# A long convolution by matmul: spectra stored in pairs of two words, first stage on 128 rows with a block-diagonal table

## The chip, the cores and the metric

The kernel runs on one core of a Trainium2 chip. A core has a matrix engine (TensorE, PE in the profile, with its weight loads shown apart as PEld), a vector engine (VectorE, DVE), a scalar engine (ScalarE, ACT), GpSimd (POOL), and queues for DMA transfers, here those of SyncE (SP) and ScalarE. The metric is device time in microseconds of one execution, lower is better; of the kernel before, three runs were timed.

## What is computed

A layer norm, a gated long convolution of 2048 positions over 512 channels, and an MLP behind a second layer norm:

```python
def _A_ref(q, k, v, shift_k, ssm_k, ssm_D):          # q is layernorm(x)
    ...
    for t in range(ks):                              # ks = 4
        k_shift = k_shift + k_pad[:, t:t + S, :] * shift_k[:, ks - 1 - t][None, None, :]
    kv = k_shift * v
    L = 2 * S
    ...                                              # zero padding to L, rfft of kv and of ssm_k
    y_f = kv_f * kf_f[None, :, :, :]
    y = irfft(y_f, L)[:, 0, :S, :]                   # shortened
    y = y + kv * ssm_D[None, None, :]
    return q * y
...
h = x + _A_ref(_layernorm(x, axis=-1), A_k, A_v, A_shift_k, A_ssm_k, A_ssm_D)
h2 = h + _B_ref(_layernorm(h, axis=-1), B_w1, B_w2)  # relu(z @ w1) @ w2, width 1376
```

## The kernel before

The Fourier transforms are written as matmuls in two stages each (a number of positions is split into 32 by 64). All instructions are issued in an order written out by hand; each engine works its own list in that order, and waits only for what it reads or overwrites.

*Setup (to about 16 us).* VectorE and ScalarE make sine and cosine tables. The small one, 64 columns, is kept as a sum of two bf16 tables, `f1hi` and `f1lo` (L192 to L195); a larger one, `st`, serves the second stage. `to_rows` (L217) transposes the filter with TensorE (L222) into `kfl`, whose partitions are four channel groups by 32 coarse positions, with 128 channels by 64 fine positions on each; here the moving operand is read 32 words apart. ACT and VectorE copy the result out of PSUM in turn.

*First stage (`stage1`, L230).* The 512 channels lie as four groups `rg` of 32 partitions. For each pair of channels and each `rg`, a matmul with 32 rows of weights (out of `kfl`, or `xfl` for the data) moves the 64 columns of `f1hi` or `f1lo`. The four `rg` use four row strips of the array side by side (`tile_position`). Eight calls each do 64 matmuls; each call fills two PSUM tiles of two banks, and each tile is written out by two instructions of 512 elements, one of VectorE and one of ScalarE (L248 and L250 for the filter, where `dmask` adds the direct term D, L252 and L253 for the data). For the data the moving table is padded to 128 columns (`wide`).

For the filter, `stage1` alternates with `taps` (L259): 8 matmuls of 512 columns for the four-tap shift convolution, and a product with `v` on VectorE (L266). Then the result is transposed by `to_rows` again, and `stage1` runs over it.

*The spectra.* The filter's are in `BK`, the data's in `BX`, both 16384 words of four bytes on each partition. A channel group g (0 to 63; each partition half holds one channel of the pair) and a first-stage frequency k1 (0 to 31) are found at

```python
BK = bkp.tile([P, 2, 2, DC, 32, 32], F32R, tag="K", name="BK")   # part, g // 32, rg, k1, g % 32
```

so 32 groups of the same k1 lie side by side, and two frequencies of the same group are 32 words (128 bytes) apart.

*Second stage and product.* `pairs(k1)` (L320) and `sums(k1)` (L329) multiply by the table `st` (or sums of it, `sm`). The weights are the tables, side by side in memory; the moving operand is one k1 of `BK` or `BX`, 256 columns: 8 runs of 32 words. `pairs` has 64 rows of weights, two matmuls at once; `sums` 128 rows. ScalarE copies the filter's part out of PSUM (`forms`, L317), and VectorE multiplies it with the data's part (`times`, L340), writing back over `BK` and `BX` at that k1. The sixteen rounds have two `pairs` and one `sums` each.

*Inverse, first stage (`inv1`, L446).* Here the spectra are the weights: for a group g the 128 weights are four `rg` by 32 k1, and they are read 32 words apart. The moving operand is a table of 256 columns (`inv3`, `inv12`). Four groups, 12 matmuls, fill one PSUM tile of two banks, of which there are three. Two copies take each tile out (L457): both by ScalarE for even blocks b, one by ScalarE and one by VectorE for odd ones. Between the sixteen blocks other work is issued: column means of `w1` on TensorE (`pm`, L434) and their subtraction on VectorE (L439), layer norm statistics and normalisation (L403, L424), and further tables.

*The rest.* When `inv1` has read `BK` for the last time its memory becomes `M`, and the loads of `w2` and of the second half of `x` start. `inv2` (L534), `gate` (L516) and the MLP (`mlp1`, L546, `mlp2`, L559) follow for four quarters of the positions.

Of the kernel before, what the change touches and what calls it, by code (L numbers as in the profile page):

```python
# [56 lines left out]
def kernel(  # L57
# [118 lines left out]
    _turns(nc, t3[:, 1, :], r3[:], n2c[:], 64, False)  # L176
    f1f = small([64], F32)
    _sin(f1f[:, 0:32], t1[:, 0:32], 128)
    _sin(f1f[:, 32:64], t1[:, 32:64], 128, neg=True)
# [20 lines left out]
    dmask = early.tile([P, DC, 64], BF16, name="dmask")  # L200
    nc.gpsimd.memset(dmask[:], 0.0)
    for dp in range(2):
        row = slice(64 * dp, 64 * dp + 1)
        nc.gpsimd.tensor_copy(out=dmask[row, :, :],
                              in_=draw[row, :].rearrange("p (r g d) -> p r g d", r=DC, d=2)[:, :, :, dp])
    nc.gpsimd.tensor_single_scalar(out=st[:, :, 128:192], in_=st[:, :, 0:64].bitcast(F32), scalar=-1.0, op=ALU.mult)
# [7 lines left out]
    def bank2(name):  # L214
        return psum.tile([P, 2, 512], F32, tag="ps", name=name)
# [13 lines left out]

    def stage1(fl, B, gb, dmul=None, wide=False):  # L230
        pss = [bank2("ps1") for _ in range(2)]
        for gi in range(8):
            g = 8 * gb + gi
            w = 128 if wide and gi < 7 else 64
            for f, first in ((f1hi, True), (f1lo, False)):
                for rg in range(4):
                    rows = slice(32 * rg, 32 * rg + 32)
                    nc.tensor.matmul(out=pss[rg // 2][:, rg % 2, 64 * gi:64 * gi + w],  # L238
                                     lhsT=fl[rows, 2 * g:2 * g + 2, :].rearrange("p d n -> p (d n)"),
                                     rhs=f[rows, 0:w], start=first, stop=not first,  # L240
                                     tile_position=(32 * rg, 0), skip_group_check=True)
        gs = slice(8 * gb, 8 * gb + 8)
        gh, gl = gb // 4, slice(8 * (gb % 4), 8 * (gb % 4) + 8)
        for h in range(2):
            rs = slice(2 * h, 2 * h + 2)
            pv = pss[h][:].rearrange("p r (g h c) -> p h r c g", h=2, c=32)
            if dmul is not None:
                nc.vector.tensor_tensor(out=B[:, 0, gh, rs, :, gl], in0=pv[:, 0],  # L248
                                        in1=dmul[:, rs, gs].unsqueeze(2).to_broadcast([P, 2, 32, 8]), op=ALU.add)
                nc.scalar.copy(out=B[:, 1, gh, rs, :, gl], in_=pv[:, 1])  # L250
            else:
                nc.scalar.copy(out=B[:, 0, gh, rs, :, gl], in_=pv[:, 0])  # L252
                nc.vector.tensor_copy(out=B[:, 1, gh, rs, :, gl], in_=pv[:, 1])  # L253

# [46 lines left out]
    BX = bxp.tile([P, 2, 2, DC, 32, 32], F32R, tag="X", name="BX")  # L301
    for gb in range(8):
        stage1(xfl, BX, gb, wide=True)
    pl.pop("psF")
# [15 lines left out]
    def pairs(k1):  # L320
        ps = psum.tile([P, 2, 512], F32, tag="u", name="u")
        for x, B in enumerate((BK, BX)):
            for i, t in ((0, st[:, k1, 64:192]), (1, st[:, k1, 0:128])):
                for dp, pq in enumerate(halves):
                    nc.tensor.matmul(out=ps[:, dp, 256 * x:256 * x + 256], lhsT=t[pq], rhs=B[pq, i, :, :, k1, :].rearrange("p h r l -> p (h r) l"),  # L325
                                     start=(i == 0), stop=(i == 1), tile_position=(64 * dp, 0), skip_group_check=True)
        return ps, forms(ps), BK[:, :, :, :, k1, :].rearrange("p s h r l -> p s (h r) l")

    def sums(k1):  # L329
        ps = psum.tile([P, 2, 512], F32, tag="u", name="us")  # L330
        for x, B in enumerate((BK, BX)):
            for j in range(2):
                for i in range(2):
                    nc.tensor.matmul(out=ps[:, j, 256 * x:256 * x + 256], lhsT=sm[:, i, k1 + j, :], rhs=B[:, i, :, :, k1 + j, :].rearrange("p h r l -> p (h r) l"),  # L334
                                     start=(i == 0), stop=(i == 1), skip_group_check=True)
        return ps, forms(ps), BX[:, 0, :, :, k1:k1 + 2, :].rearrange("p h r k l -> p k (h r) l")

    def times(unit):
        ps, kt, o = unit
        nc.vector.tensor_tensor(out=o, in0=ps[:, :, 256:512].rearrange("p s (x l) -> p s x l", l=32),  # L340
                                in1=kt[:].rearrange("p s (x l) -> p s x l", l=32), op=ALU.mult)

# [103 lines left out]
    def inv1(b):  # L446
        ps = psum.tile([P, 4, 2, 2, 64], F32, tag="ps", name="psi1")
        for i in range(4):
            g = 4 * b + i
            nc.tensor.matmul(out=ps[:, i].rearrange("p d a n -> p (d a n)"), lhsT=BX[:, 0, g // 32, :, :, g % 32].rearrange("p r k -> p (r k)"),  # L450
                             rhs=inv3[:].rearrange("p d a n -> p (d a n)"), start=True, stop=False, skip_group_check=True)
            for dp in range(2):
                nc.tensor.matmul(out=ps[:, i].rearrange("p d a n -> p (d a n)"),  # L453
                                 lhsT=BK[:, dp, g // 32, :, :, g % 32].rearrange("p r k -> p (r k)"),
                                 rhs=inv12[:, 2 - 2 * dp:6 - 2 * dp, :].rearrange("p a n -> p (a n)"),
                                 start=False, stop=(dp == 1), skip_group_check=True)
# [186 lines left out]
```

## Time and profile before

| | us |
|---|---|
| median of three runs | 250.69 (249.88 to 250.73) |
| the profiled execution | 252.94 |
| its span, first to last instruction | 251.2 |
| TensorE matmuls busy | 221.9 (88%), 2608 of them |
| TensorE weight loads busy | 160.8 (64%) |
| VectorE busy | 141.9 (56%) |
| ScalarE busy | 98.9 (39%) |
| GpSimd busy | 65.3 (26%) |
| mean granted TensorE clock | 0.955 of full |

Matmuls are pipelined, so a busy TensorE can still be waiting inside a matmul, for its weights for example; how far apart the starts of matmuls lie says more than the busy share. In the slices of the span, each a fortieth (6.28 us), a digit is the busy share in tenths:

```profile
PE   0579987758999997999999975999999999999992
PEld 0555447547888887899999975744474465444440
DVE  6859994764888885644533119307996228135031
ACT  3454443663777673243352200075027104504500
...
PEclk9999999997999998899999977599999999999998
```

The weight loads are densest from slice 16 to slice 23, which is `inv1`, and the granted clock falls at four places.

### The profile page before, as it was taken

To read this page: it belongs to the slowest core of one execution; us is meant where nothing else is said; L and a number is where in the kernel's file an instruction comes from. 1 tells how busy PE (TensorE), PEld (TensorE's weight loads), DVE (VectorE), ACT (ScalarE), POOL (GpSimd) and SP (SyncE) were. 2 spreads that over 40 slices of the span, in tenths; PEclk is the share of its full clock that TensorE was granted. 3 is DMA by queue.
4 is the path that set the end of the run, shared out by engine and by line. 5 is a ranking of instruction groups with operands and counts; after the bars stand their busy time and mean duration, and the time that the engine had idled before them with its cause. 6 is when DMAs were issued, how large, how long until landed. Compare 5 with 4: busy or idle time off the path is not lost.

```text
span 251.2 us, 6062 instructions
## 1 busy us (share of the span) xinstructions
PE 221.9 (88%) x2608; PEld 160.8 (64%) x2608; DVE 141.9 (56%) x236; ACT 98.9 (39%) x166; POOL 65.3 (26%) x80
## 2 busy tenths in 40 slices
PE   0579987758999997999999975999999999999992
PEld 0555447547888887899999975744474465444440
DVE  6859994764888885644533119307996228135031
ACT  3454443663777673243352200075027104504500
POOL 7599999910000003302230000214021000202000
PEclk9999999997999998899999977599999999999998
DMA  7999910006000002940000086994736720311011
GB/s 220 262 207 150 153 33 1 5 3 227 4 0 3 0 3 67 185 84 4 0 0 0 0 231 167 143 194 83 144 76 127 97 60 18 71 38 48 0 38 47
DMA packets 48655, 20.04 MB, mean 80 GB/s; under 512 B 43666, under 2 KB 47092, under 8 KB 48628
## 3 DMA queue, kind: packets, MB, share of 16 engines
q1 hardware_dynamic: 46688, 18.24, 36.4%
q10 hardware_dynamic: 1940, 1.42, 2.2%
q8 instruction: 20, 0.33, 0.6%
q14 instruction: 7, 0.06, 0.1%
HBM read 7.02 MB, written 2.10 MB: 36 GB/s over the span
## 4 chain that ended last, share of the span: by engine, by line
PE 87%; DVE 5%; DMA 3%; issue 2%; ACT 1%; ACTq 0%
PE ps1m L546 16%; PE ps2m L559 15%; PE psi L453 11%; PE pz L534 8%; PE u L325 8%; PE us L334 8%; PE pkv L263 6%; PE psi L450 6%; PE ps L238 4%; PE pst L222 4%; DMA E<-in_A_ssm_k_dram 3%; DVE BX L253 3%; PE pm L434 1%; ACT BX L252 1%; DVE E L266 0%
## 5 line engine op out<-in xcount | busy, mean ns | idle before, releaser
L548 ACT ACTIVATE M<-ps1m 128x512 bf16<-128x512 f32 (+1 forms) x44 | 25.9, 596 | 64.2 <-PE ps1m L546 64.2
L453 PE MATMUL psi<-inv,BK 128*128 128x256 f32 x128 | 39.3, 389 | 0.0
L559 PE MATMUL ps2m<-M 128*128 128x512 bf16 (+1 forms) x176 | 38.7, 379 | 0.0
L453 PEld LDWEIGHTS psi<-inv,BK 128*128 128x128 f32 x128 | 34.7, 318 | 0.0
L546 PEld LDWEIGHTS <-w 128*128 128x128 bf16 (+1 forms) x176 | 17.7, 102 | 20.9 <-issue 1.9
L559 PEld LDWEIGHTS <-M 128*128 128x128 bf16 (+1 forms) x176 | 17.2, 98 | 20.8
L407 POOL TENSOR_SCALAR rstd<-mv 128x4 f32<-128x4 f32 x8 | 2.4, 295 | 95.7 <-DVE mv L405 95.7
L450 PE MATMUL psi<-inv,BX 128*128 128x256 f32 x64 | 25.2, 394 | 1.4 <-DVE BX L340 1.4
L340 DVE TENSOR_TENSOR BK<-u,kt 128x512 fp32r<-128x512 f32 x32 | 20.6, 686 | 8.3 <-PE us L334 8.3
L210 ACT CAST BX<-psi 128x512 fp32r<-128x512 f32 x16 | 9.4, 587 | 32.2 <-PE psi L453 32.2
L450 PEld LDWEIGHTS psi<-inv,BX 128*128 128x128 f32 x64 | 20.2, 316 | 1.8 <-DVE BX L340 1.6
L546 PE MATMUL ps1m<-xT,w 128*128 128x512 bf16 (+1 forms) x88 | 20.7, 398 | 0.0
L562 DVE SCALAR_TENSOR_TENSOR M<-ps2m,rstd,M 128x512 bf16<-128x512 f32 x8 | 6.0, 751 | 24.0 <-PE ps2m L559 24.0
L546 PE MATMUL ps1m<-M,w 128*128 128x512 bf16 (+1 forms) x88 | 19.3, 379 | 0.0
L222 PE MATMUL pst<-identw,E 128*128 128x128 f32 x64 | 9.8, 324 | 10.4 <-DMA E<-in_A_ssm_k_dram 9.1
L212 DVE CAST ax<-psi 128x512 fp32r<-128x512 f32 x8 | 5.5, 688 | 23.8 <-ACT BX L210 23.8
L317 ACT COPY kt<-u 128x512 f32<-128x512 f32 x32 | 17.4, 587 | 3.6 <-PE u L325 2.3
L290 POOL TENSOR_TENSOR sm<-st 64x2048 fp32r<-64x2048 f32 x4 | 18.4, 4604 | 0.3
L325 PE MATMUL u<-BK,st 64*128 64x256 f32 x128 | 15.0, 312 | 2.1 <-DVE BX L253 2.1
L222 PEld LDWEIGHTS pst<-identw,E 128*128 128x128 f32 x64 | 9.4, 204 | 10.9 <-issue 9.1
L534 PE MATMUL pz<-ecore,BX 32*128 32x256 f32 (+7 forms) x128 | 12.2, 370 | 4.3 <-issue 2.9
L534 PEld LDWEIGHTS pz<-ecore,BX 32*128 32x128 f32 x128 | 10.8, 285 | 4.7 <-issue 3.1
(99 smaller groups left out, 401.2 us busy)
## 6 DMA issues: line engine op xcount, KB each, us to landing
E<-in_A_ssm_k_dram SPq DMA_DIRECT2D x1, 2048.0 KB, 8.3
out_dram<-M SPq DMA_DIRECT2D x64, 32.0 KB, 1.6
w<-in_B_w_dram SPq DMA_DIRECT2D x1, 1376.0 KB, 6.1
M<-in_B_w_dram ACTq DMA_DIRECT2D x1, 1280.0 KB, 10.9
xh<-in_A_q_dram SPq DMA_DIRECT2D x8, 128.0 KB, 2.9
M<-in_A_q_dram SPq DMA_DIRECT2D x8, 128.0 KB, 8.3
M<-in_B_w_dram ACTq DMA_DIRECT2D x1, 96.0 KB
E<-in_A_v_dram SPq DMA_TRANSPOSE x4, 5.8
```

Of the source, the lines that this page charges most:

```text
L222: nc.tensor.transpose(out=pst[:, i, :], in_=srcw[:, :, 8 * h + i], identity=identw[:])
L290: nc.gpsimd.tensor_tensor(out=sm[pq, i, :, 64 * dp:64 * dp + 64], in0=st[pq, :, 64:128].bitcast(F32), in1=st[pq, :, 0:64].bitcast(F32), op=op)
L317: nc.scalar.copy(out=kt[:], in_=ps[:, :, 0:256])
L325: nc.tensor.matmul(out=ps[:, dp, 256 * x:256 * x + 256], lhsT=t[pq], rhs=B[pq, i, :, :, k1, :].rearrange("p h r l -> p (h r) l"), start=(i ...
L334: nc.tensor.matmul(out=ps[:, j, 256 * x:256 * x + 256], lhsT=sm[:, i, k1 + j, :], rhs=B[:, i, :, :, k1 + j, :].rearrange("p h r l -> p (h ...
L340: nc.vector.tensor_tensor(out=o, in0=ps[:, :, 256:512].rearrange("p s (x l) -> p s x l", l=32), in1=kt[:].rearrange("p s (x l) -> p s x l" ...
L450: nc.tensor.matmul(out=ps[:, i].rearrange("p d a n -> p (d a n)"), lhsT=BX[:, 0, g // 32, :, :, g % 32].rearrange("p r k -> p (r k)"), rhs ...
L453: nc.tensor.matmul(out=ps[:, i].rearrange("p d a n -> p (d a n)"), lhsT=BK[:, dp, g // 32, :, :, g % 32].rearrange("p r k -> p (r k)"), rh ...
L534: nc.tensor.matmul(out=pz[:, rg, j:j + w, :].rearrange("p a b -> p (a b)"), lhsT=ax[rho][rows, n2, :, :].rearrange("p g d -> p (g d)"), rh ...
L546: nc.tensor.matmul(out=ps1[:fsz, :].rearrange("p (i t) -> p i t", i=4), lhsT=w1[:, c, fc * P:fc * P + fsz], rhs=hT[sc][:, :, c, :], start= ...
L548: nc.scalar.activation(out=h1T[:fsz, fc, :], in_=ps1[:fsz, :], func=ACT.Relu)
L559: nc.tensor.matmul(out=ps2[:], lhsT=h1T[:ksz, fc, i * P:(i + 1) * P], rhs=w2[:ksz, fc, :], start=(fc == 0), stop=(fc == NFC - 1))
```

## The change

The order of the words of `BK` and `BX` becomes: part, pair of groups (g // 2), rg, k1, g % 2. So two groups of the same k1 lie side by side, and the next k1 follows 2 words (8 bytes) further. Readers and writers of the spectra change accordingly: the moving operand of `pairs` and `sums` is now 128 runs of 2 words, 64 words apart; the weights of `inv1` are read 2 words apart; the products are written in runs of 2 words.

`stage1` no longer uses row strips. The tables `f1hi` and `f1lo` become block-diagonal, with 256 columns: the 64 columns for `rg` hold the table on that group's 32 partitions, and zeros elsewhere. One matmul with all 128 rows of weights and 256 columns then does what four with 32 rows and 64 columns did. A call covers four groups g, has 8 matmuls, fills one PSUM tile and is written out by two instructions of 512 elements; there are sixteen calls for each spectrum instead of eight, `taps` follows every second one, and the padding `wide` is gone. The tables take eight small copies in place of two, and `dmask` gets the new order.

```diff
-    BK = bkp.tile([P, 2, 2, DC, 32, 32], F32R, tag="K", name="BK")
+    BK = bkp.tile([P, 2, 32, DC, 32, 2], F32R, tag="K", name="BK")
...
-    f1hi = early.tile([P, P], BF16, name="f1_hi")
-    f1lo = early.tile([P, P], BF16, name="f1_lo")
+    f1hi = early.tile([P, DC, 64], BF16, name="f1_hi")
+    f1lo = early.tile([P, DC, 64], BF16, name="f1_lo")
     for f in (f1hi, f1lo):
-        nc.gpsimd.memset(f[:, 64:128], 0.0)
-    nc.vector.tensor_copy(out=f1hi[:, 0:64], in_=f1f[:])
-    f1d = small([64], F32)
-    nc.vector.tensor_tensor(out=f1d[:], in0=f1f[:], in1=f1hi[:, 0:64], op=ALU.subtract)
-    nc.vector.tensor_copy(out=f1lo[:, 0:64], in_=f1d[:])
+        nc.gpsimd.memset(f[:], 0.0)
+    f1h = small([64], BF16)
+    nc.vector.tensor_copy(out=f1h, in_=f1f)
+    nc.vector.tensor_tensor(out=f1d, in0=f1f, in1=f1h, op=ALU.subtract)
+    for rg in range(DC):
+        rows = slice(32 * rg, 32 * rg + 32)
+        nc.vector.tensor_copy(out=f1hi[rows, rg, :], in_=f1f[rows, :])
+        nc.vector.tensor_copy(out=f1lo[rows, rg, :], in_=f1d[rows, :])
...
-    def stage1(fl, B, gb, dmul=None, wide=False):
-        pss = [bank2("ps1") for _ in range(2)]
-        for gi in range(8):
-            g = 8 * gb + gi
-            w = 128 if wide and gi < 7 else 64
-            for f, first in ((f1hi, True), (f1lo, False)):
-                for rg in range(4):
-                    rows = slice(32 * rg, 32 * rg + 32)
-                    nc.tensor.matmul(out=pss[rg // 2][:, rg % 2, 64 * gi:64 * gi + w],
-                                     lhsT=fl[rows, 2 * g:2 * g + 2, :].rearrange("p d n -> p (d n)"),
-                                     rhs=f[rows, 0:w], start=first, stop=not first,
-                                     tile_position=(32 * rg, 0), skip_group_check=True)
...
+    def stage1(fl, B, t, dmul=None):
+
+        ps = bank2("ps1")[:].rearrange("p a (r l x) -> p a r l x", r=DC, l=2)
+        for a in range(2):
+            for gl in range(2):
+                g = 4 * t + 2 * a + gl
+                for f, first in ((f1hi, True), (f1lo, False)):
+                    nc.tensor.matmul(out=ps[:, a, :, gl, :], lhsT=fl[:, 2 * g:2 * g + 2, :].rearrange("p d n -> p (d n)"),
+                                     rhs=f[:], start=first, stop=not first, skip_group_check=True)
+        gp = slice(2 * t, 2 * t + 2)
+        pv = ps.rearrange("p a r l (h c) -> p h (a r) c l", h=2)
+        o = [B[:, i, gp].rearrange("p a r c l -> p (a r) c l") for i in range(2)]
+        if dmul is not None:
+            nc.vector.tensor_tensor(out=o[0], in0=pv[:, 0], in1=dmul[:, gp].rearrange("p a r l -> p (a r) l").unsqueeze(2)
+                                    .to_broadcast([P, 8, 32, 2]), op=ALU.add)
+            nc.scalar.copy(out=o[1], in_=pv[:, 1])
+        else:
+            nc.scalar.copy(out=o[0], in_=pv[:, 0])
+            nc.vector.tensor_copy(out=o[1], in_=pv[:, 1])
...
-    for gb in range(8):
-        stage1(kfl, BK, gb, dmask)
-        taps(gb // 2, gb % 2)
+    for t in range(16):
+        stage1(kfl, BK, t, dmask)
+        if t % 2 == 1:
+            taps(t // 4, t // 2 % 2)
...
-                    nc.tensor.matmul(out=ps[:, dp, 256 * x:256 * x + 256], lhsT=t[pq], rhs=B[pq, i, :, :, k1, :].rearrange("p h r l -> p (h r) l"),
+                    nc.tensor.matmul(out=ps[:, dp, 256 * x:256 * x + 256], lhsT=t[pq], rhs=B[pq, i, :, :, k1, :].rearrange("p a r l -> p (a r) l"),
...
-            nc.tensor.matmul(out=ps[:, i].rearrange("p d a n -> p (d a n)"), lhsT=BX[:, 0, g // 32, :, :, g % 32].rearrange("p r k -> p (r k)"),
+            nc.tensor.matmul(out=ps[:, i].rearrange("p d a n -> p (d a n)"), lhsT=BX[:, 0, g // 2, :, :, g % 2].rearrange("p r k -> p (r k)"),
```

More of the change, by code (lines that the diff above doesn't have):

```diff
@@ L177 @@
     f1f = small([64], F32)
+    f1d = small([64], F32)
     _sin(f1f[:, 0:32], t1[:, 0:32], 128)
@@ L199 @@
                                 in1=wsh[:, rg, :].unsqueeze(2).to_broadcast([P, KS, P]), op=ALU.mult)
-    dmask = early.tile([P, DC, 64], BF16, name="dmask")
+    dmask = early.tile([P, 32, DC, 2], BF16, name="dmask")
     nc.gpsimd.memset(dmask[:], 0.0)
@@ L203 @@
         row = slice(64 * dp, 64 * dp + 1)
-        nc.gpsimd.tensor_copy(out=dmask[row, :, :],
-                              in_=draw[row, :].rearrange("p (r g d) -> p r g d", r=DC, d=2)[:, :, :, dp])
+        nc.gpsimd.tensor_copy(out=dmask[row].rearrange("p a r l -> p r a l"),
+                              in_=draw[row, :].rearrange("p (r a l d) -> p r a l d", r=DC, l=2, d=2)[:, :, :, :, dp])
     nc.gpsimd.tensor_single_scalar(out=st[:, :, 128:192], in_=st[:, :, 0:64].bitcast(F32), scalar=-1.0, op=ALU.mult)
@@ L228, in to_rows @@
                                            scalar=0, op=ALU.bitwise_or)
-    def stage1(fl, B, gb, dmul=None, wide=False):
-        pss = [bank2("ps1") for _ in range(2)]
-        for gi in range(8):
-            g = 8 * gb + gi
-            w = 128 if wide and gi < 7 else 64
-            for f, first in ((f1hi, True), (f1lo, False)):
-                for rg in range(4):
-                    rows = slice(32 * rg, 32 * rg + 32)
-                    nc.tensor.matmul(out=pss[rg // 2][:, rg % 2, 64 * gi:64 * gi + w],
-                                     lhsT=fl[rows, 2 * g:2 * g + 2, :].rearrange("p d n -> p (d n)"),
-                                     rhs=f[rows, 0:w], start=first, stop=not first,
-                                     tile_position=(32 * rg, 0), skip_group_check=True)
[L242 to L253, printed above, removed]
@@ L300 @@
         to_rows(vT, h, xfl[:])
-    BX = bxp.tile([P, 2, 2, DC, 32, 32], F32R, tag="X", name="BX")
-    for gb in range(8):
-        stage1(xfl, BX, gb, wide=True)
+    BX = bxp.tile([P, 2, 32, DC, 32, 2], F32R, tag="X", name="BX")
+    for t in range(16):
+        stage1(xfl, BX, t)
     pl.pop("psF")
@@ L333, in sums @@
                 for i in range(2):
-                    nc.tensor.matmul(out=ps[:, j, 256 * x:256 * x + 256], lhsT=sm[:, i, k1 + j, :], rhs=B[:, i, :, :, k1 + j, :].rearrange("p h r l -> p (h r) l"),
+                    nc.tensor.matmul(out=ps[:, j, 256 * x:256 * x + 256], lhsT=sm[:, i, k1 + j, :], rhs=B[:, i, :, :, k1 + j, :].rearrange("p a r l -> p (a r) l"),
                                      start=(i == 0), stop=(i == 1), skip_group_check=True)
@@ L339, in times @@
         ps, kt, o = unit
-        nc.vector.tensor_tensor(out=o, in0=ps[:, :, 256:512].rearrange("p s (x l) -> p s x l", l=32),
-                                in1=kt[:].rearrange("p s (x l) -> p s x l", l=32), op=ALU.mult)
+        nc.vector.tensor_tensor(out=o, in0=ps[:, :, 256:512].rearrange("p s (x l) -> p s x l", l=2),
+                                in1=kt[:].rearrange("p s (x l) -> p s x l", l=2), op=ALU.mult)
     for k1 in range(0, 32, 2):
@@ L453, in inv1 @@
                 nc.tensor.matmul(out=ps[:, i].rearrange("p d a n -> p (d a n)"),
-                                 lhsT=BK[:, dp, g // 32, :, :, g % 32].rearrange("p r k -> p (r k)"),
+                                 lhsT=BK[:, dp, g // 2, :, :, g % 2].rearrange("p r k -> p (r k)"),
                                  rhs=inv12[:, 2 - 2 * dp:6 - 2 * dp, :].rearrange("p a n -> p (a n)"),
```

## The prediction

> **What bounds the kernel now.** I read the stretches first, cut where the chain of work changes its kind, then that chain, then the groups of instructions, then the order of time where a stretch gets shorter. The columns of the stretches are the stretch, its length, the busy time of PE, PEld, DVE, ACT and POOL, the granted clock, the DMA share and GB/s.
>
> ```profile
> 16.40:37.80 21.40, 20.05 (x576) 10.44 (x576) 19.46 (x24) 10.07 (x17) 20.86 (x18) 1.00 0.91 123
> 43.00:57.70 14.70, 9.03 (x512) 7.45 (x513) 10.12 (x16) 8.50 (x16) 8.38 (x2) 1.00 0.07 12
> 57.70:97.80 40.10, 38.73 (x384) 33.97 (x384) 31.37 (x48) 26.84 (x48) 0.00 (x0) 0.96 0.09 34
> 97.80:145.80 48.00, 46.55 (x212) 45.04 (x212) 19.50 (x36) 15.76 (x28) 9.65 (x19) 0.96 0.23 46
> 145.80:161.00 15.20, 12.35 (x256) 12.11 (x257) 8.14 (x16) 0.00 (x0) 1.27 (x2) 0.64 0.84 204
> ```
>
> The rows are: first stage of the filter with the taps, first stage of the data, second stage with the products, `inv1`, and `inv2(0)` with `inv2(1)`. TensorE is the bound in all but the second. The chain gives start and length:
>
> ```profile
> 16.44 0.68 PE ps L238 x64
> 17.12 1.84 PE pkv L263 x8
> 18.95 0.61 PE ps L238 x64
> ...
> 57.72 1.83 PE u L325 x16
> 59.56 2.00 PE us L334 x8
> 61.56 1.16 PE u L325 x16
> 62.72 1.16 PE us L334 x8
> ...
> 121.68 0.60 PE pm L434 x4
> ...
> 123.14 0.45 PE psi L453 x2
> 123.59 0.23 PE psi L450
> ...
> 151.63 2.85 issue
> ```
>
> In `inv1` a matmul starts every 0.45/2 = 224 ns, although its 256 columns are as many as those of `us` (8 in 1.16 us). The weight loads tell why:
>
> ```profile
> L453 PEld LDWEIGHTS psi<-inv,BK 128*128 128x128 f32 x128 | 34.7, 318 | 0.0
> L334 PEld LDWEIGHTS us<-BX,sm 128*128 128x128 f32 x64 | 9.2, 198 | 0.0
> L222 PEld LDWEIGHTS pst<-identw,E 128*128 128x128 f32 x64 | 9.4, 204 | 10.9 <-issue 9.1
> ```
>
> Same size and type; `inv1` takes its 128 weights at a step of 32 words, the other two side by side. 318 against 198 ns is a load that sets the cadence: 224 ns a load, 1.75 ns a word.
>
> **The change, part by part.**
>
> *1. Weights of `inv1` at a step of two words.* The step goes from 128 to 8 bytes. No row has a step of 2, so I bound it: from below by side-by-side loads, which leave the matmul as the bound. Four quarter-array matmuls of `inv2` side by side go every 119 ns (a full-clock `inv2` on the chain has 32 such groups in 3.80 us); within `u`, four matmuls, two and two at once, take 71.37 to 71.61, 120 ns a pair. From above by 224 ns, nothing won. I take 118 ns, because 8 bytes are far nearer to 4 than to 128: if a lone word costs one access of 1.75 ns, and an access brings the neighbour too, two words are 0.88 ns each and 128 are 112 ns, just below the matmul's 118. That gives 192 x (224 - 118) = -20.4 us on TensorE.
>
> The Trainium skill, page "Advanced Engine Details and Errata", section "SBUF Cachelines", says that SBUF works in pieces of 16 bytes and that two hits on a piece absorb the access; the row at a step of 32 words agrees with the penalty, and none shows two hits. By this rule the load is at full rate and this part is worth the -17.4 below; by the rows alone it could be anything down to 0.
>
> Not all of it arrives, because VectorE and its queue now matter. It has 19.5 us of work in the 48, and its copies out of PSUM (one for every odd block of `inv1`) stand behind normalisation work:
>
> ```profile
> 102.33 2.47 DVE L403 BATCH_NORM_STATS2 st<-xh 128x6 f32<-128x512 bf16 x4 [4.54 <-DMA xh<-in_A_q_dram]
> 106.18 0.69 DVE L212 CAST ax<-psi 128x512 fp32r<-128x512 f32 x1 [0.45 <-ACT BX L210]
> ```
>
> A block is now 12 x 118 = 1.42 us, with three PSUM buffers. Laid out by hand: the loads of `xh` still land at 102.3, block 1 is copied at about 107, so block 4, which could start at 105.8, waits 1.3 us; block 10 waits 1.5 us for block 7's copy behind the second statistics (2.46 + 0.36 us). With 0.3 for the last copy, 3 us come back. ACT's 15.8 us fit in 29. Net -17.4 (both ends: -20.4 and 0).
>
> *2. First stage of the filter, full array.* For each period of 64 small matmuls and 8 taps the chain takes 2.51 us (34.04 - 16.44 over seven). The 64 become 16 of 256 columns in bf16. `pm`, 344 columns with full bf16 loads, goes at 0.60/4 = 150 ns; by columns that is 112 ns; 8 taps of 512 columns at 9.51/44 = 216 ns (`ps2m`, L559) are 1.73, since no change of array shape stands between them any more. 16 x 0.112 + 1.73 = 3.52; 8 x (3.52 - 2.51) = +8.1 us. Bounds: 16 x 0.108 (half a 512-column one) and 16 x 0.119, +7.5 to +9.0. VectorE's 2 x 0.68 + 1.23 = 2.6 us a period lies under 3.5; it was the cover before.
>
> The Trainium skill, page "TensorEngine Tiling (Array Packing)", section "When to Use Tiling", speaks against this part: a contraction of 32 rows calls for four row tiles, and giving them up costs up to four times. The row shows 64 in about 0.5 to 0.6 us, four times that is 2.0 to 2.4 a period, and the sum by the rule would be some 2 to 5 us higher than mine.
>
> *3. First stage of the data.* Evictions (VectorE 685, ACT 591 ns, 16 each, as before) set it, with waits: 14.6 us. Now 128 x 112 = 14.3 us on TensorE plus one last pair of evictions, 0.59 + 0.69 + 0.1 = 15.7: +1.1 (0 to +2).
>
> *4. Clock at the start of the second stage.* The first `u` and `us` take 1.83 + 2.00 instead of 2 x 1.16 us. TensorE had little to do in the 3.5 us ahead (evictions, and 0.81 us of issue at 54.2). With a dense first stage only 1.4 us are idle, as at 36.5 and 41.7, where no slow stretch follows: -1.5 (0 to -1.5).
>
> *5. Second stage: the moving operand in runs of two words,* 256 bytes apart, before of 32. Nearest row: the transposes at L222 move 128 single words 128 bytes apart; 32 take 3.87 us, 121 ns each with their start. So a lone word costs at most 0.95 ns on this side, and 128 runs at most 121 ns, level with today's 118 to 120. I take 0. From above, a jump and a hit added: 0.95 + 0.46 (118/256) is 1.41 a run, 180 ns, over 256 slots (128 pairs of `u`, 128 of `us`) +16 us; from below 0. The rates differ between weight and moving side, so this is my least sure zero.
>
> *6. Products and evictions in other strides.* VectorE's 48 products write runs of two words. Rows with runs of eight cost the plain length (682 ns, L248). Taken 0; covered up to 2.33/3 = 0.777 us a product, as three share a period of 2.33 us; now 0.69. The first-stage evictions write solid blocks: 0.
>
> *7. Setup.* Eight small casts (186 ns each) instead of two: 1.1 us on VectorE ahead of 16.4, where it waits for transposes (4.96 busy of 7.3): 0, or +1 if that cover is gone. The wider memsets lie on POOL while it waits for `wsh`: 0.
>
> *8. After `inv1`* the loads of `x` and `w2` (11.2 us on SP's queue) start when BK is free, thus 17 us earlier, and all hangs on that point as before. The 2.85 us of issue at 151.6 fall together with a 16 KB instruction packet at 151.8, behind these loads; TensorE then runs at half clock. I take 0: the same instructions meet the same loads. If the packet slips ahead: 2.85 us and most of the half clock are won (12.35 us of matmuls here against 2 x 3.80 later): 2.85 and, since `gate(0)` and the transposes still follow, some two thirds of 4.75, together -6.
>
> **Sum.** -17.4 + 8.1 + 1.1 - 1.5 = -9.7. The profiled execution took 252.94 us (span 251.2, 1.7 around it): 243.2. The median of the runs is 250.69, 2.25 lower, so on it 241.0.
>
> **Rivals.**
> - *A: any step but one is dear to weights.* Part 1 falls away: +8.1 + 1.1 - 1.5 = +7.7, 258.4. For it: the trace has only steps 1 and 32. This is also the case that the change doesn't do what it says.
> - *B: the moving operand pays in the second stage.* Slower than before once a slot costs 9.7/256 = 38 ns more; with the bound above +16, 257. For it: this side has to bring 256/118 = 2.2 words a nanosecond, twice what the weights get; against it the transposes.
> - *C: the products pay.* From 0.777 us each; at twice today's 0.69, 48 x 1.38 = 66 us for a stretch of 37: +29, 270. Against it: every VectorE row follows its element count.
> - *D: half the weight penalty stays,* (224 + 112)/2 = 168 ns: 192 x 50 = 9.6 less, of which the 3 us of waits vanish: 247.6.
> - *E: the tail clears up* (part 8): 241.0 - 6 = 235.
>
> **How the numbers follow.** Forecast 0.55, A 0.10, B 0.09, C 0.05, D 0.07, E 0.14. Under 0.5%, 1.25 us, a measurement of this kernel tells nothing; 0.02 each of B and D fall there. Faster: 0.55 + 0.14 + 0.05 = 0.74; same 0.04; slower 0.10 + 0.07 + 0.05 = 0.22. Predicted is the forecast's 241. Its own range is 236 to 245: part 2's and 3's bounds +-2, part 1's waits +-2, part 4's 1.5. The range from 232 (E with the low bounds) to 252 leaves out A, C and the greater part of B, some 0.2.
>
> **What would show it.** `inv1` weight loads of about 190 to 200 ns and a matmul every 118 ns; L325 and L334 cadences unchanged; a period of 3.5 us in the filter's first stage; a first `u` at 1.16 us; the `inv1` stretch near 30 us with two short waits on VectorE's copies. Wrong if those loads stay at 318 ns (A), if matmuls of `u` start more than 150 ns apart (B), if TensorE waits for L340 (C).

## The result, and the profile after

The changed kernel takes 285.19 us (median of four runs, 283.51 to 287.62), the kernel before 250.71 on the same chip: 1.1395 times as long, interval 1.1274 to 1.1516. Slower by 34.5 us, where 9.7 less had been forecast. The profiled execution took 284.02 us, its span 282.2, 31.0 more than before. The profiled execution of the kernel before, at 252.94 us, was one of its slower ones, so some 2 us between the two traces belong to that execution and not to the change.

Cutting both traces at the first instruction of each stage shows where the 31 us lie:

| stage | before, us | after, us | difference | forecast |
|---|---|---|---|---|
| setup, to the first `ps` | 16.4 | 16.1 | -0.4 | 0 |
| filter's first stage and taps | 21.4 | 29.3 | +7.9 | +8.1 |
| transposes of the product | 5.3 | 5.3 | 0 | 0 |
| data's first stage | 14.6 | 15.6 | +1.0 | +1.1 |
| second stage and products | 40.1 | 83.8 | +43.7 | -1.5 |
| `inv1` | 47.9 | 29.8 | -18.1 | -17.4 |
| `inv2(0)` and `inv2(1)` | 15.2 | 13.6 | -1.6 | 0 |
| the rest | 90.2 | 88.8 | -1.4 | 0 |

One row is wrong by 45 us; no other is off by more than 1.6. First the stretches of the changed kernel, in the same columns as before (stretch, length, busy time of PE, PEld, DVE, ACT, POOL, granted clock, DMA share, GB/s), for the filter's first stage, the data's, the second stage, and most of `inv1`:

```profile
16.05:45.30 29.25, 27.76 (x188) 18.68 (x192) 19.68 (x24) 9.79 (x17) 28.50 (x21) 1.00 0.49 90
50.60:66.20 15.60, 14.13 (x128) 12.43 (x128) 11.06 (x16) 9.38 (x16) 2.07 (x1) 1.00 0.03 5
66.20:150.00 83.80, 82.39 (x384) 69.93 (x384) 46.44 (x48) 28.70 (x48) 0.00 (x0) 0.52 0.05 17
150.00:177.00 27.00, 26.97 (x198) 25.37 (x199) 18.62 (x35) 13.87 (x25) 9.62 (x19) 0.90 0.36 79
```

In the third line the second stage runs the same 384 matmuls in twice the time; TensorE is busy for all but 1.4 us of it: no other engine holds it up between its matmuls, and the time lies inside them. Now the chain of waits, with start and length:

```profile
19.68 1.75 PE ps L241 x16
21.43 1.73 PE pkv L262 x8
...
66.24 2.55 PE u L325 x16
68.79 2.47 PE us L334 x8
71.27 2.58 PE u L325 x13
...
150.62 0.43 PE psi L453 x2
...
152.97 2.32 PE pm L434 x8
...
163.23 0.12 PE psi L450
163.35 0.24 PE psi L453 x2
...
184.15 3.17 issue
```

The first two lines are the period of the filter's first stage, 1.75 + 1.73 = 3.48 us (3.52 forecast). `u` and `us` take 2.47 to 2.58 us where they took 1.16: a slot is the distance between the starts of two matmuls of 256 columns (for `u` two matmuls at once count as one), eight of them last about 2.3 us, and some 0.25 us is added where a unit gives way to the next. A matmul of `us` starts every 287 to 291 ns, not every 118 to 120. In `inv1` one goes every 0.24/2 = 120 ns, as forecast. The clock and the groups of instructions of the same kernel (the groups give busy time and mean ns of one):

```profile
PEclk9999999999555555555555999968999999999999
```

```profile
L453 PEld LDWEIGHTS psi<-inv,BK 128*128 128x128 f32 x128 | 21.2, 205 | 0.0
...
L334 PEld LDWEIGHTS us<-BX,sm 128*128 128x128 f32 x64 | 18.9, 317 | 0.2
...
L340 DVE TENSOR_TENSOR BK<-u,kt 128x512 fp32r<-128x512 f32 x32 | 35.4, 1143 | 36.1 <-PE us L334 36.1
```

The weights of `inv1` load in 205 ns instead of 318: a step of two words is as good as side by side. The loads at L334 have become as long as those of `inv1` were, 317 ns, although their weights are read as before. They don't set the cadence here: with the same weights and a solid moving operand they take 188 ns (L336 of the run with a solid moving operand, below), so they have grown along with the matmuls. The products at L340 take 1143 ns on average instead of 0.69 us.

Two things here invite a wrong reading. The granted clock is half from 70.1 to 155.4 us, and the product is slow. But the first `u`, and the first half of the first `us`, ran ahead of that, in slices of full clock, and took the same 2.55 and 2.47 us: the clock doesn't make the second stage long. The first `u` ran ahead of the first product, too (VectorE starts it at 69.6 us). And the product's idle time is put down to `us`: it waits for TensorE, not TensorE for it. The half clock costs something only where the next stage begins: the first twelve matmuls of `inv1` go every 213 ns instead of 120, and `pm` in its first block takes 2.32 us for 8, where 4 take 0.60 at full clock; some 2.2 us together. The trace before, whose clock is half there for a while as well, has in its chain at the same place

```profile
100.86 2.00 PE pm L434 x8
```

so against it some 1.2 us are new.

### The profile page after: what moved, and what is told of

The parts are those of the page before. It is cut to its first block, busy times and chain, and to the rows that moved or that the text cites. A ratio compares the mean times of both kernels' runs of the same rounds, so it can differ in the third digit from the quotient of the medians.

```text
span 282.2 us, 4526 instructions
## 1 busy us (share of the span) xinstructions
PE 255.9 (91%) x1832; PEld 188.6 (67%) x1840; DVE 159.7 (57%) x243; ACT 101.5 (36%) x166; POOL 67.6 (24%) x80
## 4 chain that ended last, share of the span: by engine, by line
PE 89%; DMA 3%; issue 2%; POOL 2%; DVE 2%; ACT 1%; POOLq 0%
PE u L325 15%; PE us L334 15%; PE ps1m L546 14%; PE ps2m L559 13%; PE ps L241 10%; PE pz L534 6%; PE psi L453 6%; PE pkv L262 5%; PE psi L450 3%; DMA wsh<-in_A_shift_k_dram 3%; POOL E L202 2%; PE pst L226 1%; PE pm L434 1%; DVE E L265 0%; DVE xfl L231 0%
## 5 line engine op out<-in xcount | busy, mean ns | idle before, releaser
L340 DVE TENSOR_TENSOR BK<-u,kt 128x512 fp32r<-128x512 f32 x32 | 35.4, 1143 | 36.1 <-PE us L334 36.1
L546 PEld LDWEIGHTS <-w 128*128 128x128 bf16 (+1 forms) x176 | 17.4, 100 | 19.9
L325 PE MATMUL u<-BK,st 64*128 64x256 f32 x128 | 26.9, 510 | 1.5 <-DVE BX L252 1.5
L325 PE MATMUL u<-BX,st 64*128 64x256 f32 x128 | 24.7, 474 | 0.0
L453 PE MATMUL psi<-inv,BK 128*128 128x256 f32 x128 | 24.3, 291 | 0.0
L334 PE MATMUL us<-BK,sm 128*128 128x256 f32 x64 | 23.8, 514 | 0.0
L325 PEld LDWEIGHTS u<-BK,st 64*128 64x128 f32 x128 | 17.5, 305 | 7.4 <-issue 7.3
L334 PE MATMUL us<-BX,sm 128*128 128x256 f32 x64 | 21.5, 478 | 0.0
L453 PEld LDWEIGHTS psi<-inv,BK 128*128 128x128 f32 x128 | 21.2, 205 | 0.0
L334 PEld LDWEIGHTS us<-BK,sm 128*128 128x128 f32 x64 | 16.5, 308 | 6.1 <-issue 6.0
L325 PEld LDWEIGHTS u<-BX,st 64*128 64x128 f32 x128 | 19.4, 310 | 0.1
```

The costliest lines, as they stand in the source:

```text
L546: nc.tensor.matmul(out=ps1[:fsz, :].rearrange("p (i t) -> p i t", i=4), lhsT=w1[:, c, fc * P:fc * P + fsz], rhs=hT[sc][:, :, c, :], start= ...
```

## The experiments

Theory 1: a moving operand in runs of two words is read word by word, at a price for each word whatever the clock and the writers do. Rivals: the full-array first stage leaves the chip in a state (clock, PSUM) that makes the second stage slow (2); the products' writes disturb the reads (3).

### Streams of equal matmuls in one pattern

One kernel holds nothing but streams of 16 equal matmuls, each stream with another pattern for the moving operand, the weights or a transpose; the layer is left out, and the output is zeros. Between them stand 20 matmuls on a solid operand. The core of it:

```diff
+    def mov(name, rhs, n=16, w=None):
+        ps = pp.tile([P, 2, 512], F32, tag="ps", name=name)
+        for i in range(n):
...
+            nc.tensor.matmul(out=o, lhsT=W[:, 0:128], rhs=rhs, start=True, stop=True, skip_group_check=True)
...
+    mov("mSolid", runs(X, 256, 256)); warm()
+    mov("mRunTwoStepE", runs(X, 2, 64)); warm()
+    mov("mRunFourStepB", runs(X, 4, 8)); warm()
```

> This kernel computes nothing of the reference (its output is zeros); it holds streams of 16 equal matmuls, each stream with another access pattern of the moving operand (256 fp32r columns) or of the weights (128), and between them a stream of solid matmuls. In the changed kernel a slot of the second stage (256 columns as 128 runs of 2 words, 256 bytes apart) takes 285 to 290 ns instead of 118. Three theories. Bank: the distance of 256 bytes sends every run to the same part of the memory; then runs of 2 at 264, 272 or 288 bytes go at about 118 to 130 ns, at 256 and 512 bytes at 285 or more, and single words at 260 bytes faster than at 256. Piece: two words of each 16-byte piece are too few for the moving side, whatever the distance; then runs of 2 at 264, 272, 288 and 128 bytes all take 285, and runs of 4 some 118 to 145. Short run: every new run costs the address counter the same; then runs of 2 are slow even 16 bytes apart, and runs of 4 and 8 cost a half and a quarter of the loss. Weights: step 1 and 2 at 112 ns, step 32 at 224; whether step 4 is at 112 or 224 says if a lone word per piece is what costs. Transposes (single words): 112 ns at 128 bytes; at 256 bytes over 200 by Bank, 112 by the other two. Product of VectorE: runs of two alone 0.69 us by Bank, and slower only while TensorE reads runs at the same place of each 256 bytes.

The chain of waits of this kernel: `m` is a pattern of the moving operand, `w` of the weights, `t` of a transpose's moving operand; then come the length of a run and a letter for its distance. The cadences in the text are the median distance between the starts of a stream's matmuls; the length of a stream over its 16 matmuls comes within 7 ns of them.

```profile
19.92 1.92 PE mSolid L99 x16
...
28.52 3.63 PE mRunTwoStepA L99 x16
...
53.38 4.64 PE mRunTwoStepE L99 x16
...
66.81 3.63 PE mRunTwoStepG L99 x16
...
98.11 3.50 PE mRunOneStepD L99 x16
...
104.00 4.59 PE mRunOneStepE L99 x16
108.59 3.56 PE warm L89 x20
...
118.55 1.89 PE mRunFourStepB L99 x16
...
127.56 2.34 PE mRunFourStepI L99 x16
...
160.08 1.83 PE wStepTwo L105 x16
...
164.37 3.67 PE wStepFour L105 x16
...
201.53 1.81 PE tStepD L110 x16
...
223.09 12.93 PE mSameTime L99 x44
```

A solid operand gives a slot of 120 ns. Runs of two give 227 ns when they lie 16 bytes (StepA) or 272 bytes (StepG) apart, and 291 at the 256 bytes of the change (StepE). Single words are no dearer than runs of two: 219 ns at 128 bytes (OneStepD), 287 at 256 (OneStepE). So the second word of a run isn't free: 227/256 = 0.89 ns for each word, in company or alone. Runs of four are free at 32 bytes (119 ns, FourStepB) and at 528 (120, FourStepJ), and take 147 ns at 512 (FourStepI). Weights of 128 words load in 111 ns side by side, 118 at a step of two words, 233 at four: on that side two words of each 16 bytes are enough, here they aren't. The transpose with single words 128 bytes apart (tStepD) takes 113 ns, one with its words side by side 109; 113/128 = 0.88 ns a word, the price of a lone word.

None of the three theories holds alone. Runs of two are slow at every distance, against Bank; but 256 bytes make them slower still, against Piece and Short run; and runs of four, free at 32 bytes, keep no half of the loss, against Short run. What fits is a price by the piece and a second one by the distance (transposes at 256 bytes take 148 ns, neither 112 nor over 200).

The end of the same kernel has VectorE's product alone and beside TensorE. In the order of time (start, length, then the instruction):

```profile
221.45 0.69 DVE L158 TENSOR_TENSOR X<-dSource,kt 128x512 fp32r<-128x512 f32 x1
...
224.48 1.85 DVE L163 TENSOR_TENSOR X<-dSource,kt 128x512 fp32r<-128x512 f32 x1
...
226.89 0.69 DVE L165 TENSOR_TENSOR X<-dSource,kt 128x512 fp32r<-128x512 f32 x1
```

The three write runs of two, 256 bytes apart: with TensorE idle (0.69 us), while TensorE reads runs of two at the same place of each 256 bytes, in another tile (1.85 us), and with the writes moved by half of the 256 bytes (0.69). So writers are hurt by the reads, and by the place they share, not by a shared word. The reads aren't hurt by the writes: in `mSameTime`, the stream beside these products, a matmul starts every 289 ns, as during the products so after them, and without any writer it was 291.

### The first stage alone

The old layout with the full-array first stage; the result goes into the spectra in runs of four words.

```diff
-    BK = bkp.tile([P, 2, 32, DC, 32, 2], F32R, tag="K", name="BK")
+    BK = bkp.tile([P, 2, 2, DC, 32, 32], F32R, tag="K", name="BK")
...
-        ps = bank2("ps1")[:].rearrange("p a (r l x) -> p a r l x", r=DC, l=2)
+        ps = bank2("ps1")[:].rearrange("p a (l r x) -> p a l r x", r=DC, l=2)
...
-        o = [B[:, i, gp].rearrange("p a r c l -> p (a r) c l") for i in range(2)]
+        o = [B[:, i, gh, :, :, gl] for i in range(2)]
```

> The old layout of the spectra with the new first stage alone (128 rows, block-diagonal table). My terms: +8.1 for the filter's first stage, +1.1 for the data's, up to -1.5 for the clock behind it, second stage and inv1 as before: about 258 us, 256 to 260. Rival: if the array's change of shape is what made the second stage of the changed kernel slow (half clock behind a dense first stage), this kernel shows it too, with u at 2.5 us and about 300 us in all.

257.74 us, 1.0336 times before (1.0265 to 1.0407): 7.2 us more than the 250.58 measured beside it, and +7.7 had been worked out. The chain of waits at the start of its second stage:

```profile
67.26 1.24 PE u L326 x16
68.50 1.15 PE us L335 x8
```

The dense first stage leaves the second at its old cadence, so rival 2 falls. It also shows the clock's term, which nothing else could: the first `u` and `us` take 1.24 and 1.15 us where they took 1.83 and 2.00, and the stage 38.7 us where it took 40.1, -1.4 (forecast -1.5). The first stages cost 29.3 - 21.4 and 15.6 - 14.6 us, as in the changed kernel.

### The changed kernel with a solid moving operand

The second stage moves 256 words side by side out of the table instead of the spectra; so its products aren't the layer's. All else is the changed kernel, the products' writes included.

```diff
+    solid = st[:].rearrange("p a b -> p (a b)")
...
-rhs=B[pq, i, :, :, k1, :].rearrange("p a r l -> p (a r) l"),
+rhs=solid[pq, 4 * k1:4 * k1 + 256],
...
-rhs=B[:, i, :, :, k1 + j, :].rearrange("p a r l -> p (a r) l"),
+rhs=solid[:, 4 * k1:4 * k1 + 256],
```

> The changed kernel, but the second stage moves 256 words of the table st that lie side by side, in place of the spectra (it leaves the spectra out of the second stage; all else, the products in runs of two included, is as in the changed kernel). If the moving operand's runs of two are the whole loss: a slot of L325 and L334 back at 118 ns, 256 slots x 169 ns = 43 us less, the clock full in that stage, products of VectorE back near 0.69 us, and some 241 us in all, which is what was predicted for the change. Rival: half clock or the products' writes hold the stage; then u stays above 1.8 us a unit and the total above 260.

236.61 us, 0.9453 times before (0.9376 to 0.953). Its second stage in the chain of waits:

```profile
67.00 1.21 PE u L327 x16
68.21 1.14 PE us L336 x8
```

The pattern of the reads was taken away, and with it went the long matmuls, the half clock and the slow products (687 ns). The reads also go to another tile here, so this run alone couldn't tell the pattern from the waits between reads and products; the next one can, as it reads the same tile in runs. Rival 3 falls by three rows together: the writes are the same here and cost nothing, the streams have slots of 291 ns without any writer and 289 with one, and in the changed kernel the first `u` was as slow ahead of the first product. This is also the sum of all the other steps, with no price on the moving operand: 14.5 us less than before, where -9.7 had been worked out.

### Runs of two, not 256 bytes apart

As above, but runs of two words 144 bytes apart.

```diff
+    def apart(pq, k1):
+        return solid[pq, 4 * k1:4 * k1 + 4608].rearrange("p (x s) -> p x s", s=36)[:, :, 0:2]
...
-rhs=B[pq, i, :, :, k1, :].rearrange("p a r l -> p (a r) l"),
+rhs=apart(pq, k1),
```

> The changed kernel, with the second stage moving words of the table st in place of the spectra, as in the solid run, but in 128 runs of two words, 144 bytes apart (it leaves the spectra out of the second stage). It splits the loss of a slot in the kernel: by the probe, runs of two cost 227 ns where the distance is no multiple of 128 or 256 bytes, and 60 ns more at 256. So the slot here should be 227 ns, the second stage 256 x 113 = 29 us longer than with the solid operand (114 ns), and the total 265 us, 263 to 268. Rival: in the kernel the short run alone is the whole loss; then 285 ns and 280 us. Other rival: place alone is the loss; then 118 ns and 237 us. VectorE's products: 0.69 us if only reads at the products' own places slow them.

266.82 us, 1.0686 times before (1.0534 to 1.0838). Its chain of waits:

```profile
81.17 2.02 PE us L339 x8
83.19 2.01 PE u L330 x14
```

A unit takes 2.02 us instead of 1.14 with the solid operand, (2.02 - 1.14)/8 = 110 ns a slot; the changed kernel's 2.58 are another 70. So of the 180 ns that a slot lost there against the solid operand, 110 come from reading word by word and 70 from the distance of 256 bytes (107 and 64 in the streams, where no unit ends). Over the stage it is 66.3 us against 37.9 with the solid operand and 83.8 in the changed kernel: 28.4 and 17.5 us. The products take 692 ns here. The clock is half for one short stretch, 68.6 to 72.1 us, and full in the rest of the stage (0.972 over the span). The long half clock thus goes, in these two kernels, with slots of 287 to 291 ns and not with those of 227 to 232.

### Which runs are read at full rate

A second kernel of streams, again without the layer: runs that begin in the middle of 16 aligned bytes, longer ones, and bf16 operands.

```diff
+    mov("mFourSolidAligned", runs(X, 4, 8)); warm()
+    mov("mFourOffByTwo", runs(X, 4, 8, at=2)); warm()
+    mov("mEightOffByTwo", runs(X, 8, 16, at=2)); warm()
...
+    movb("bTwo", runsb(2, 4)); warm()
+    movb("bOne", runsb(1, 2)); warm()
+    movb("bTwoFar", runsb(2, 64)); warm()
```

> Computes nothing of the reference (output zeros); streams of 16 equal matmuls. If the moving side needs the whole 16-byte piece: runs of four that begin in the middle of a piece cost more than aligned ones (118), nearer to 227 ns; runs of eight begun there lie between; solid operands lose nothing. Runs of six (252 words) lie between 118 and 227. If only the length of the run counts, where it begins is without effect. In bf16 (2 bytes) runs of 8 or more are at full rate (108 to 112 ns); runs of 4 and 2 tell whether bytes or elements count: by bytes runs of 4 (8 bytes) are slow like two words. VectorE's product in runs of two while TensorE reads runs of four at the same place: over 0.69 us; half of 256 bytes away: 0.69.

The chain of waits of this kernel:

```profile
19.67 1.89 PE mFourSolidAligned L99 x16
...
23.94 3.63 PE mFourOffByTwo L99 x16
...
36.05 2.67 PE mEightOffByTwo L99 x16
...
74.45 1.83 PE bTwo L130 x16
...
78.67 1.83 PE bOne L130 x16
...
82.89 3.48 PE bTwoFar L130 x16
```

Four words in one aligned piece of 16 bytes take 119 ns a slot, the same four begun in the middle of a piece 227: for fp32 words it is the whole piece that counts, not the length of the run. Runs of eight off by two have one whole piece and four loose words: (4 x 0.46 + 4 x 0.89)/8 x 256 = 173 ns, measured 167. Runs of six have two loose words in six: 3.62/6 x 252 = 152, measured 150. In bf16, where a piece holds eight elements, four of them are enough: every second element, or two of every four, is nearly free (bOne and bTwo, 113 ns, 109 solid), while two elements out of 128 bytes aren't (218). That speaks for four elements of a piece, whatever their size, rather than for all of its bytes. VectorE's product beside a stream of runs of four at the same place takes 1.76 to 1.78 us, and 0.69 half of 256 bytes away, as with runs of two.

### Runs of four words

If a whole piece is what counts, both readers can be served: four words side by side for the moving operand, two words apart for the weights. The tile keeps the shape of the change, [part, 2, 32, rg, k1, g % 2], with another meaning for its words: for one k1, two `rg` by two groups lie side by side, 512 bytes from the next four; the weights of `inv1` for one group are still 128 words at a step of two. The order of the table's columns (even k1 first) makes it so. The first stage is the one of before, with four row strips. The direct term D is added to the first column of the filter, so that both evictions are plain copies. The whole reference is computed.

```diff
+    def four(B, pq, i, k1):
+        v = B[pq, i].rearrange("p a (h e) q l -> p (a h) e (q l)", h=2)
+        return v[:, :, k1 % 2, 4 * (k1 // 2):4 * (k1 // 2) + 4]
...
-    nc.gpsimd.iota(r1[:], pattern=[[2, 32]], base=1, channel_multiplier=0)
+    nc.gpsimd.iota(r1[:].rearrange("p (e q) -> p e q", e=2), pattern=[[2, 2], [4, 16]], base=1, channel_multiplier=0)
...
+                o = B[:, i, 4 * gb:4 * gb + 4].rearrange("p a (h e) q l -> p a h (e q l)", h=2)[:, :, h]
+                copy(eng, o.rearrange("p a (c r l) -> p a c r l", r=2, l=2), pv[:, i])
```

> First stage of before (row strips); the spectra lie so that the moving operand of one k1 has runs of four words, 512 bytes apart, and the products so that the weights of inv1 are still 2 words apart; D goes into the filter's first tap instead of dmask. By the probe: slot 147 ns (+7.4 us against 118), inv1 at 118 to 120 ns (-18 us against before), first stage as before: about 240 us. If VectorE's product at the place that TensorE reads takes 1.6 us as in the changed kernel, it has 1.6 + 0.69 + 0.69 = 3.0 us a period against TensorE's 2.8, and the total is 243. Rival (it is not the length of the run): the slot stays near 285 ns and the total near 276.

235.82 us, 0.9408 times before (0.9347 to 0.9469): it beats both kernels. The stretches of its second stage and of `inv1`:

```profile
56.86:104.00 47.14, 45.53 (x384) 39.33 (x384) 32.52 (x48) 28.87 (x48) 0.00 (x0) 0.93 0.08 29
104.00:132.90 28.90, 27.49 (x212) 26.07 (x212) 19.22 (x36) 15.52 (x28) 9.57 (x19) 0.94 0.36 76
```

`inv1` gains as in the changed kernel (28.9 us against 47.9), the first stages cost nothing (21.7 and 14.2 us, 21.4 and 14.6 before), and the second stage loses 7.0 (47.1 against 40.1), because runs of four 512 bytes apart pay for that distance: in the chain a unit is 1.36 us against 1.16, (1.36 - 1.16)/8 = 25 ns a slot, 256 x 25 = 6.4 us; the streams had 147 - 119 = 28. These two stages come as expected, -19.0 and +7.0 us where -18 and +7.4 had been worked out. That the whole is 4 us below the 240 expected lies elsewhere, for the most part in `inv2(0)` and `inv2(1)`: 10.7 us here, 15.2 before, and 12.3 with the first stage alone, where nothing behind the first stage was changed. That part isn't shown to come from the layout.

```profile
79.35 1.36 PE us L328 x8
80.72 1.36 PE u L319 x16
```

### Its products out of the way of the reads

In that kernel a product on `BK` takes 754 ns on average: the first of each round 820 to 854, the second some 670. The suspicion is that TensorE reads at the same place of each 256 bytes during the first. Here `sums` multiplies the data first, so that what TensorE reads during that product lies elsewhere.

```diff
-        for x, B in enumerate((BK, BX)):
+        for x, B in ((1, BX), (0, BK)):
```

> As the runs of four, but sums(k1) multiplies the data before the filter, so that the first product, which waits for the last read of BK at k1, starts when TensorE has gone on to other words. If the slow product comes from reads and writes at the same place of each 256 bytes, it goes back to 0.69 us and the total is 2 to 3 us below the run before, 240; if not, the two are equal, or this one is slower by the later product (3 us).

242.9 us, 0.9725 times before (0.966 to 0.9791), and 7.1 us more than with the other order: a miss. The product does go back to 686 ns, so the place was its cause. But it can't start before both parts are there, and PSUM tiles come free later. A round of its second stage in the order of time, with the wait and what ended it in brackets:

```profile
72.63 1.29 DVE L334 TENSOR_TENSOR BK<-u,kt 128x512 fp32r<-128x512 f32 x2 [1.17 <-PE us L328]
...
73.38 0.30 PEld L319 LDWEIGHTS u<-BK,st 64*128 64x128 f32 x4 [0.34 <-DVE BK L334]
...
74.14 0.58 PEld L328 LDWEIGHTS us<-BX,sm 128*128 128x128 f32 x4 [0.19 <-DVE BK L334]
```

VectorE waits 1.17 us for TensorE, and TensorE's next loads then wait for VectorE, 0.34 and 0.19 us here; up to 104 us the groups of instructions show 5.1 and 2.6 us of such waits, and none with the other order. The stage takes 51.6 us instead of 47.1. The other part of the loss, 4.7 us in `inv2(0)` and `inv2(1)`, is the issue near their start, which is 5.0 us here and 2.9 there, and what follows it (6.2 us against 3.6), with the half clock behind it; why it differs between the two wasn't tried.

## Why the prediction was wrong

By its own parts:

1. *Weights of `inv1`*: right in its main term, with luck in the rest. -17.4 forecast, -18.1 measured; 120 ns a matmul (118 taken), loads of 205 ns (190 to 200). The matmuls alone give 192 x 105 = -20.2; of the 3 us that waits on VectorE's copies were to take back, the trace has one wait of some 0.3 us (at 162.3, on ScalarE), and of the 2.1 that did come back the half clock at the start of the stage accounts for some 1.2. So the waits were priced too high, and the clock hid it. With the clock full, behind the solid operand, the stage takes 28.2 us, and two waits on VectorE are there, as forecast, but of some 0.6 us in all. The rule cited there from the Trainium skill, page "Advanced Engine Details and Errata", section "SBUF Cachelines" (two hits on a 16-byte piece absorb the access), holds for the weights: 118 ns for 128 words at a step of two, 111 side by side.
2. *First stage of the filter*: right, +7.9 for +8.1, and a period of 3.48 us for 3.52. Four times the price for giving up row strips, which the prediction held against itself, would have been 2 to 5 us too much; 16 full matmuls took 1.75 us where 64 small ones took 0.61 to 0.74, some 2.4 to 2.9 times as much.
3. *First stage of the data*: right, +1.0 for +1.1.
4. *Clock*: right, -1.4 for -1.5, but seen only in the first stage alone; in the changed kernel it is lost in the second stage.
5. *Moving operand in runs of two*: this step failed. It was taken as 0 and measured +43.7 us with the clock's gain in it, some 45 by itself: 32 units x (2.58 - 1.16). The sentence that failed is "a lone word costs at most 0.95 ns on this side, and 128 runs at most 121". The price of the lone word was nearly right (0.88 to 0.89). But it was charged once for a run, and the runs show it charged for each of the 256 words, unless a whole aligned 16-byte piece is taken: 256 x 0.89 = 227 ns. The row of the transposes couldn't have told: with 128 single words it takes 113 ns, and 109 solid, so at that size the solid form is no faster, and the price doesn't show. The bound from above, 180 ns, made the same mistake once more, with 0.46 ns for the second word. The case that the moving operand pays was therefore priced at 257 instead of 285 and, at a chance of 0.09, far too unlikely. The rule on 16-byte pieces would have allowed this step (two hits on each piece); no run here agrees with it for the moving operand: 227 ns for two words out of each piece, 119 for all four.
   On top, 60 to 70 ns a slot come from the distance of 256 bytes. The trace before couldn't show it: its own second stage moves runs 4096 bytes apart, a multiple of 256, too, but only 8 of them of 32 words, and such a stream takes 119 ns (mRunAfBeforeTt), as if solid.
6. *Products*: taken as 0, and that is what they cost, but for another reason than given. One third of them, the first product of each round on a tile of `pairs`, takes about 1.6 us (1609 to 1636 ns), more than the cover of 0.777 us. The period of three had grown to 5.2 us, and covers them.
7. and 8. *Setup and tail*: taken as 0; -0.4 and -3.0. The tail's issue stayed (3.17 us). The -3.0 isn't shown to be the change's: the first stage alone, with the layout of before, has 12.3 and 88.8 us there, 4.3 less than the profiled execution before.

With a solid operand in place of step 5, the same kernel took 236.61 us where the sum said 241. Its trace is 15.6 us shorter than the one before, 5.9 beyond the sum's -9.7: 2.3 in `inv1`, where the waits and the half clock are missing, 2.9 in the tail, which isn't shown to be the change's, and 0.7 in the second stage.

What stays open is why a distance of 256 bytes costs more. The streams say only where it shows: runs of two take 227 ns at 16, 233 at 32, 247 at 64, 260 at 128, 291 at 256, 287 at 512, and 251 at 264, 227 at 272, 233 at 288 bytes. That the half clock follows from TensorE being fed too slowly is a reading, too; no run changed the clock alone, and the streams are too short to tell: behind single words at 256 bytes (287 ns) the next 20 solid matmuls take 3.56 us instead of 2.40, behind runs of two at 256 bytes (291 ns) they don't.

## What to carry to other kernels

A layout that serves one reader has to be priced for the other with its own rate: the weights were content with two words of each aligned 16 bytes, the moving fp32 operand needed all four, and that difference (some 28 us), with the price of the distance on top (some 17), made 45 us against a gain of 18. Charge a price per word for each word until a row shows that neighbours are free, and mistrust a row whose solid form would take the same time, as it can't show a penalty. Where two readers want different orders, look for one in which each gets just what it needs: runs of four for one and a step of two for the other made it 5.9% faster than before, some 12 of the 15 us in the two stages that read the spectra.

## What the hardware showed that was not expected

- The moving side, in fp32, counts whole aligned 16-byte pieces: about 0.46 ns a word inside one, 0.89 outside. Runs of four words begun in the middle of a piece take 227 ns a slot, aligned 119. In bf16 four elements of a piece are enough (113 ns, 109 solid).
- Distances of 256 and 512 bytes cost short runs extra: runs of two 287 to 291 ns against 227, runs of four 147 against 119 to 120, and 16 bytes more (272, 528) take it away. Runs of 32 words 4096 bytes apart pay nothing (119).
- VectorE's writes slow down from 0.69 to between 1.55 and 1.85 us while TensorE reads runs at the same place of each 256 bytes in another tile; half of 256 bytes away they take 0.69.
- TensorE's granted clock went to half for 85 us while its matmuls took 287 to 291 ns a slot, though TensorE was busy all the time; at 227 ns a slot it was half for 3.4 us of the stage. A slot was as long before the clock fell as after.
